# Masking attention scores with a bitwise AND on VectorE, and moving GpSimd's products and low halves of the attention to VectorE

## The chip, the cores and the metric

The kernel runs on one core of a Trainium2 chip. The metric is the device time of one execution in microseconds (us). Engines are named as in the profile: PE is TensorE's matrix multiplication and PEld its weight load, DVE is VectorE, ACT is ScalarE, POOL is GpSimd, SP is SyncE, which only issues DMA transfers here.

## The reference

Three layers follow each other, on 2 sequences of 768 tokens with a model width of 384 (8 heads of 48):

```python
for t in range(S):                       # linear attention with decay
    cur = einsum('bhd,bhe->bhde', u * k[t], v[t])
    y[t] = einsum('bhd,bhde->bhe', r[t], state + cur)
    state = w[t][..., None] * state + einsum('bhd,bhe->bhde', k[t], v[t])
...
u = x + real(fft(fft(x, axis=1), axis=2))          # mixture layer, width 4 * 384
out = u + relu(layernorm(u) @ w_ch1) @ w_ch2
...
h = gelu(x @ w_in); u, v = split(h)                # gated layer, width 1024
out = x + (u * (w_sg @ (layernorm(v) * g) + b_sg)) @ w_out
```

## The kernel before

**Attention in chunks.** The 8 heads of a sequence make 4 pairs, so there are 8 pairs n = 0 to 7 in all: 0 to 3 for the first sequence, 4 to 7 for the second. A pair's 768 tokens are cut into 6 chunks of 128. Within a chunk the decays are undone by a running product, and the chunk becomes three matrix products: scores (keys by queries, of which only those with the key before the query count), the product of the masked scores and the values, and the state carried from chunk to chunk.

For each pair `prep` (lines 199 to 254) loads the decays, the stacked queries and keys (rk) and the values (v) over SP's queue. Then VectorE scans the decays (L232), ScalarE takes a logarithm and an exponential for the reciprocal (L238, L239), a product r*k is formed for the token's own term (L243, only for pairs 0 to 3), VectorE scales the queries (L245), and the keys are made in three steps: a product (L247), a correction of the reciprocal (L249) and the last step (L250). `PV` and `KV` say for which pairs VectorE makes the products of L243 and L247; GpSimd makes the others. Before, these are pair 0 and pairs 0 and 1.

`own_term` (L258 on) gives the term of a token with itself, with u in place of the decay. For pairs 0 to 3 TensorE sums r*k*u over the head (dg_ps), ScalarE copies the 12 columns out of PSUM (L274), and `times_v` multiplies the values by them on GpSimd (L279), which makes dv. For pairs 4 to 7 (`TM`) r, k and u come from memory in another order (prod), GpSimd multiplies them (L264, L266), VectorE sums (L267), and the same `times_v` follows.

`scores` (L282 on) makes three chunks at once for both heads of a pair, so it is called twice per pair and makes 4 tiles of 128x384. Each tile leaves PSUM in a copy by ScalarE (L293) and is masked by GpSimd with an affine select (L294):

```python
nc.scalar.copy(sc, sc_ps)
nc.gpsimd.affine_select(out=sc, in_=sc, pattern=[[0, 3], [1, C]], compare_op=ALU.is_gt, fill=0.0, base=0, channel_multiplier=-1)
```

`chunk_states` transposes the keys (kn), multiplies them by the values (kv_ps), copies these to us, fills dec with the chunks' decays (L317, ScalarE), runs a scan over the chunks on VectorE (L319) and copies the states to U (L321). `values` adds state and score terms in y_ps and adds dv on VectorE (L344). `butterfly` (L346 on) forms sums and differences of the two halves of the tokens (L349, L350), a rounded high half on ScalarE (L351) and the low half as the difference (L352), on GpSimd but for pair 3. The tiles kn, us and the butterfly's x share one buffer (tag "kn", one buffer): each waits until the one before has been read.

**Order.** `attention` (L354 on) runs through the pairs with the loads two pairs ahead. The work of a pair overlaps the tail (the second half of `values` and the butterfly) of the one before. After the first sequence's pairs come the Fourier steps; from there (about 104 us) `merge` interleaves the second sequence's attention with the mixture layer of the first sequence. A planner orders the instructions; each engine then runs its own in that order and waits, in order, for what they need. Manual dependencies (`behind`, `in_order`) keep the order around the end of the first sequence. PSUM has eight banks: five (gps) are taken in turn by scores, z_ps of the mixture layer and other products, and three (cps) hold some of the first sequence's tiles and later the layer's sums.

**Weights.** `convert` (L170 to L172, VectorE) unpacks a weight from 64 bits with shifts and bitwise operations; `divide` splits it into a high half (L176, ScalarE) and a low half (L177, GpSimd). One buffer (st) holds the unpacked words until GpSimd has read them.

Of the kernel before, what the change touches and what calls it, by code (L numbers as in the profile page):

```python
# [9 lines left out]
F32 = mybir.dt.float32  # L10
# [4 lines left out]
U32 = mybir.dt.uint32  # L15
# [8 lines left out]
CFGF = dict(ps=2, su=2)  # L24
KC = 9
LA = 4
KV = range(2)
NJ0 = 28
JP = -1000000
LNPE = ((0, 0),)  # L30
# [1 line left out]
STB = 1  # L32
TB = 0
XB = 1
PV = range(1)
TM = range(4, 8)
YB = 1
DB = 0
# [49 lines left out]
def strided(x, *free):  # L88

    return bass.AP(x.tensor, x.offset, [x.ap[0], *free])  # L90
# [3 lines left out]
def fused(ctx, tc, ins, out, dbg=None):  # L94
# [163 lines left out]
    def own_term(ap, n, b, p, prod, v):  # L258

        dv = ap([C, NC_, 2 * D], "dv")  # L260
        dg = ap([C, NC_, 2, 1], "dg")
        if n in TM:
            r, k, u = (prod[:, i * 2 * D * NC_:(i + 1) * 2 * D * NC_ if i < 2 else ROW].rearrange("p (c e) -> p c e", e=2 * D) for i in range(3))
            own = (nc.vector if n in PV else nc.gpsimd).tensor_tensor(out=r, in0=r, in1=k, op=ALU.mult)  # L264
            behind(own, first_through, mybir.DependencyClass.Sync)
            nc.gpsimd.tensor_tensor(out=r, in0=r, in1=u.to_broadcast([C, NC_, 2 * D]), op=ALU.mult)  # L266
            nc.vector.tensor_reduce(out=dg.rearrange("p c h o -> p (c h o)"), in_=r.rearrange("p c (h e) -> p (c h) e", h=2), op=ALU.add, axis=AX.X)  # L267
            times_v(dv, dg, v)
            return dv
        dg_ps = ps(b, [C, 512], "dg_ps", DB)  # L270
        for c in range(NC_):

            nc.tensor.matmul(dg_ps[:, 2 * c:2 * c + C], lhsT=prod[:, c], rhs=uh[:, None, 2 * p:2 * p + 2].to_broadcast([PR, C // 2, 2]), start=True, stop=True)
        nc.scalar.copy(dg[:, :, :, 0], dg_ps[:, :2 * NC_].rearrange("p (c h) -> p c h", h=2))  # L274
        times_v(dv, dg, v)
        return dv

    def times_v(dv, dg, v):
        nc.gpsimd.tensor_tensor(out=dv.rearrange("p c (h e) -> p (c h) e", h=2), in0=v.rearrange("p c (h e) -> p (c h) e", h=2),  # L279
                                in1=dg.rearrange("p c h o -> p (c h) o").to_broadcast([C, NC_ * 2, D]), op=ALU.mult)  # L280

    def scores(ap, c0, rt, kt):  # L282

        res = []
        sc_pss = [gps.tile([C, 3, C], F32, name="sc_ps", tag="g") for h in range(2)]
        for i, h in [(i, h) for i in range(3) for h in range(2)]:
            c = c0 + i

            hs = slice(64 * h, 64 * h + D)
            nc.tensor.matmul(sc_pss[h][:, i, :], lhsT=kt[hs, c * C:(c + 1) * C], rhs=rt[hs, c, :], start=True, stop=True)  # L290
        for sc_ps in sc_pss:
            sc = ap([C, 3, C], "sc")
            nc.scalar.copy(sc, sc_ps)  # L293
            nc.gpsimd.affine_select(out=sc, in_=sc, pattern=[[0, 3], [1, C]], compare_op=ALU.is_gt, fill=0.0, base=0, channel_multiplier=-1)  # L294
            res.append(sc)
        return res

    def chunk_states(ap, b, ends, kt, v, U):
# [13 lines left out]
                o = c * 2 * D + h * D  # L312
                nc.tensor.matmul(kv_ps[r0:r1, c * D:c * D + C], lhsT=kn[:, c, r0:r1], rhs=vf[:, o:o + C], start=True, stop=True)

        us = ap([PR, D, NC_], "kn")
        nc.scalar.copy(us, kv_ps[:, :NC_ * D].rearrange("p (c e) -> p e c", c=NC_))
        nc.scalar.copy(dec[:, :, 0:NC_ - 1], ends[:, None, 0:NC_ - 1].to_broadcast([PR, D, NC_ - 1]))  # L317
        chain = us.rearrange("p e c -> p (e c)")
        nc.vector.tensor_tensor_scan(out=chain, data0=chain, data1=dec.rearrange("p e c -> p (e c)"), initial=0.0, op0=ALU.add, op1=ALU.mult)  # L319
        for h, r0 in ((0, 0), (1, 64)):  # L320
# [25 lines left out]
    def butterfly(ap, y, AB, es, low):  # L346

        x = ap([C, NC_, 2 * D], "kn")
        nc.vector.tensor_tensor(out=x[:, 0:3], in0=y[:, 0:3], in1=y[:, 3:6], op=ALU.add)  # L349
        nc.vector.tensor_tensor(out=x[:, 3:6], in0=y[:, 0:3], in1=y[:, 3:6], op=ALU.subtract)  # L350
        nc.scalar.copy(AB.hi[:, :, es], x)  # L351
        low.tensor_tensor(out=AB.lo[:, :, es], in0=x, in1=AB.hi[:, :, es].bitcast(F32), op=ALU.subtract)  # L352

    def attention(ap, made, through):  # L354
# [11 lines left out]
        def tail(n, b, p, rt, sc, v, dv):  # L366
            nonlocal gate, region
            if (b, p) == (0, NP - 1):
                region = len(nc.cur_bb.bb.instructions)
            gate = values(b, 3, rt, sc[2:], v, dv, states[n % 2])  # L370
            butterfly(ap, dv, made(b), slice(p * 2 * D, (p + 1) * 2 * D), nc.vector if b == 0 and p == NP - 1 else nc.gpsimd)
            through(b, p)
            return b if p == NP - 1 else None

# [469 lines left out]
    with ExitStack() as main, ExitStack() as low, ExitStack() as late, ExitStack() as att:  # L844
# [4 lines left out]
        nc.gpsimd.memset(d1[:, :, 0:1], 1.0)  # L849
        states = [sh.tile([PR, NC_ - 1, 2 * D], F32, name=f"U{i}") for i in range(2)]  # L850
        all_ends = [sh.tile([PR, NC_], F32, name=f"ends{i}") for i in range(3)]
        dec = sh.tile([PR, D, NC_], F32, name="dec")
        for t in (*states, *all_ends, dec):
            nc.gpsimd.memset(t, 0.0)
        uh = sh.tile([PR, 2 * NP], F32, name="uh")
        dft(sh)

        def load_consts():
            nc.sync.dma_start(out=ident, in_=ins["ident"])
            nc.sync.dma_start(out=uh, in_=ins["uh"])  # L860

        a_room = room(att.enter_context(tc.tile_pool(name="att", bufs=1)), CFG1)
        f1_room = room_of(a_room, ps="v", su="dv")
# [126 lines left out]
def _constants():  # L990
# [15 lines left out]
    for i in range(2):  # L1006
# [5 lines left out]
        "fdft": _parts(fd).transpose(1, 0, 2, 3),  # L1012
        "half": half.reshape(C, 2, 2 * C),
        "ident": np.eye(C, dtype=np.float32),
    }


# [64 lines left out]
```

## Time and profile before

| | |
|---|---|
| median of 3 runs (lowest to highest) | 487.02 us (485.54 to 487.31) |
| the profiled execution's own time, and its span | 485.52 us, 483.7 us |
| PE busy | 433.6 us, 90% of the span, 2662 instructions |
| VectorE busy | 274.0 us, 57%, 453 instructions |
| ScalarE busy | 172.7 us, 36%, 369 instructions |
| GpSimd busy | 182.1 us, 38%, 182 instructions |

The span runs from the first to the last instruction. A share is an average over stages in which different engines set the pace, so it must be read together with the stretches below. A row of the timeline gives the start, the duration, engine, line, operation, and what is written from what; in brackets stands the engine's idle time before it and what ended it. PEclk is the granted clock of TensorE as a part of 2.4 GHz; 0.50 is the lower level, 1.2 GHz.

### The profile page before, as it was taken

How to read it: one execution, taken by the hardware profiler on the slowest of the kernel's cores; microseconds unless marked ns; L12 is line 12 of the kernel's file. 1: busy time of each engine (PE TensorE's matmuls, PEld its weight loads, DVE VectorE, ACT ScalarE, POOL GpSimd, SP SyncE). 2: the span in 40 equal slices, each digit the busy share in tenths (PEclk: the TensorE clock that was granted, in tenths of full speed). 3: DMA queues.
4: the chain of work that ended last, by engine and by line, in shares of the span. 5: the costliest groups of instructions: out<-in, count | busy, mean ns of one | idle time of the engine just before them, and what ended most of it. 6: DMA issues, size and time to landing. Idle time of an engine off the chain costs nothing.

```text
span 483.7 us, 6884 instructions
## 1 busy us (share of the span) xinstructions
PE 433.6 (90%) x2662; PEld 408.3 (84%) x2662; DVE 274.0 (57%) x453; ACT 172.7 (36%) x369; POOL 182.1 (38%) x182
## 2 busy tenths in 40 slices
PE   8778788876789688999999799999998999999994
PEld 8667787765678678899999699999987998999994
DVE  4857387389986978634044963541158734711332
ACT  2435355452344236444322532431355413311110
POOL 2857553154786967320000341200446524200330
PEclk9659899897979989999999899999999999999998
DMA  8948534036035223013000041000243100110002
GB/s 213 251 146 265 166 119 130 0 101 242 0 119 176 91 67 110 1 40 91 1 0 2 1 131 33 1 0 1 66 114 88 61 1 1 43 56 1 0 20 87
DMA packets 14074, 36.75 MB, mean 76 GB/s; under 512 B 1808, under 2 KB 5680, under 8 KB 13648
## 3 DMA queue, kind: packets, MB, share of 16 engines
q1 hardware_dynamic: 13456, 32.54, 22.5%
q0 software_dynamic: 576, 3.68, 2.2%
q8 instruction: 23, 0.38, 0.3%
q14 instruction: 19, 0.16, 0.1%
HBM read 33.86 MB, written 2.36 MB: 75 GB/s over the span
## 4 chain that ended last, share of the span: by engine, by line
PE 55%; DVE 15%; issue 10%; POOL 6%; DMA 5%; ACT 4%; SPq 1%; POOLq 0%; ACTq 0%; DVEq 0%
PE s_ps L107 10%; PE ch L107 8%; PE z_ps L107 8%; PE o_ps L107 5%; PE u_ps L107 4%; PE d_ps L107 3%; PE x_ps L107 3%; PE v_ps L107 3%; PE t_ps L426 2%; PE y_ps L342 2%; DMA raw<-in_wsg 2%; DVE st L171 2%; DVE st L170 2%; DVE st L172 1%; DMA w_raw<-in_w 1%
## 5 line engine op out<-in xcount | busy, mean ns | idle before, releaser
L107 PE MATMUL ch<-z_hi,w 128*128 128x384 f32 x288 | 84.5, 355 | 3.9 <-DVE uT L541 2.3
L107 PE MATMUL z_ps<-us_hi,w 128*128 128x384 f32 x288 | 82.5, 348 | 0.8 <-ACT us_hi L506 0.5
L107 PEld LDWEIGHTS ch<-z_hi,w 128*128 128x128 f32 x288 | 55.4, 199 | 6.0 <-ACT z_hi L530 2.7
L107 PE MATMUL ch<-z_lo,w 128*128 128x384 f32 x144 | 51.3, 356 | 10.2 <-DVE z_lo L531 10.2
L531 DVE SCALAR_TENSOR_TENSOR z_lo<-z_ps,z_hi 128x384 fp32r<-128x384 f32 x48 | 26.4, 552 | 55.7 <-ACT z_hi L530 55.7
L107 PEld LDWEIGHTS z_ps<-us_hi,w 128*128 128x128 f32 x288 | 54.1, 193 | 2.2 <-ACT us_hi L506 0.8
L107 PE MATMUL z_ps<-us_lo,w 128*128 128x384 f32 x144 | 49.4, 343 | 0.0
L530 ACT ACTIVATE z_hi<-z_ps 128x384 fp32r<-128x384 f32 x48 | 23.4, 490 | 57.0 <-PE z_ps L107 43.8
L107 PEld LDWEIGHTS ch<-z_lo,w 128*128 128x128 f32 x144 | 28.5, 198 | 12.4 <-DVE z_lo L531 12.1
L623 POOL TENSOR_TENSOR vn_lo<-t_g,vn_hi 128x384 fp32r<-128x384 f32 x16 | 16.1, 1014 | 57.1 <-ACT vn_hi L622 57.1
L619 DVE SCALAR_TENSOR_TENSOR t_g<-s_ps,g,bsg 128x384 f32<-128x384 f32 x16 | 9.5, 615 | 43.6 <-PE s_ps L107 43.6
L294 POOL TENSOR_SCALAR_AFFINE_SELECT sc<-sc 128x384 f32<-128x384 f32 x32 | 29.5, 939 | 12.0 <-ACT sc L293 12.0
L342 PE MATMUL y_ps<-v,sc 128*128 128x120 f32 (+1 forms) x192 | 34.0, 301 | 0.0
L177 POOL TENSOR_TENSOR w<-st,w 128x384 fp32r<-128x384 f32 (+1 forms) x18 | 24.4, 1363 | 24.0 <-ACT w L176 23.9
L107 PE MATMUL s_ps<-wsg_hi,vn_lo 128*128 128x384 f32 x96 | 32.3, 336 | 0.0
L107 PE MATMUL s_ps<-wsg_hi,vn_hi 128*128 128x384 f32 x96 | 32.3, 336 | 0.0
L107 PE MATMUL s_ps<-wsg_lo,vn_hi 128*128 128x384 f32 x96 | 32.3, 336 | 0.0
L483 POOL TENSOR_TENSOR z_lo<-uc,z_hi 128x384 fp32r<-128x384 f32 x7 | 7.8, 1120 | 60.0 <-ACT z_hi L482 59.9
L342 PEld LDWEIGHTS y_ps<-v,sc 128*128 128x128 f32 x192 | 28.6, 209 | 1.2 <-issue 0.8
L107 PEld LDWEIGHTS z_ps<-us_lo,w 128*128 128x128 f32 x144 | 27.9, 194 | 0.0
L177 POOL TENSOR_TENSOR wsg_lo<-raw,wsg_hi 128x384 fp32r<-128x384 f32 x12 | 12.4, 1038 | 33.2 <-ACT wsg_hi L176 33.2
L622 ACT CAST vn_hi<-t_g 128x384 fp32r<-128x384 f32 x16 | 8.0, 513 | 38.9 <-DVE t_g L620 28.0
(261 smaller groups left out, 1060.0 us busy)
## 6 DMA issues: line engine op xcount, KB each, us to landing
raw<-in_w SPq DMA_DIRECT2D x12, 384.0 KB, 3.4
w_raw<-in_w SPq DMA_DIRECT2D x12, 384.0 KB, 4.5
raw<-in_win SPq DMA_DIRECT2D x8, 384.0 KB, 3.8
prod<-in_ruk SPq DMA_DIRECT2D x4, 624.0 KB, 4.6
tdft<-in_tdft POOLq DMA_DIRECT2D x2, 1158.0 KB, 6.8
v<-in_v SPq DMA_DIRECT2D x8, 288.0 KB, 5.7
raw<-in_wsg SPq DMA_DIRECT2D x12, 192.0 KB, 2.4
out<-o SPq DMA_DIRECT2D x12, 192.0 KB, 1.9
```

The costliest lines, as they stand in the source:

```text
L107: nc.tensor.matmul(o, lhsT=x, rhs=y, start=start and i == 0, stop=stop and i == len(ps) - 1, **kw)
L170: behind(nc.vector.tensor_scalar(out=st, in0=top, scalar1=3, scalar2=0x3FFFFFF8, op0=ALU.logical_shift_left, op1=ALU.bitwise_and), first_t ...
L171: nc.vector.scalar_tensor_tensor(out=st, in0=top, scalar=0xC0000000, in1=st, op0=ALU.bitwise_and, op1=ALU.bitwise_or)
L177: nc.gpsimd.tensor_tensor(out=w.lo[to], in0=x, in1=w.hi[to].bitcast(F32), op=ALU.subtract)
L294: nc.gpsimd.affine_select(out=sc, in_=sc, pattern=[[0, 3], [1, C]], compare_op=ALU.is_gt, fill=0.0, base=0, channel_multiplier=-1)
L342: nc.tensor.matmul(y3[:, i, to], lhsT=sc[h][:, i, :], rhs=vf[:, of], start=c == 0, stop=True, skip_group_check=c > 0)
L426: nc.tensor.matmul(o, lhsT=l, rhs=r, start=i == 0, stop=i == len(parts) - 1)
L530: nc.scalar.activation(out=z.hi, in_=z_ps, func=AF.Relu)
L531: nc.vector.scalar_tensor_tensor(out=z.lo, in0=z_ps, scalar=0.0, in1=z.hi.bitcast(F32), op0=ALU.max, op1=ALU.subtract)
L619: nc.vector.scalar_tensor_tensor(out=t, in0=s_ps[h], scalar=g[:, f:f + 1], in1=bsg[:, hs], op0=ALU.mult, op1=ALU.add)
L622: nc.scalar.copy(vn.hi[:, f, 3 * h:3 * h + 3], th)
L623: nc.gpsimd.tensor_tensor(out=vn.lo[:, f, 3 * h:3 * h + 3], in0=th, in1=vn.hi[:, f, 3 * h:3 * h + 3].bitcast(F32), op=ALU.subtract)
```

## The change

The mask becomes a constant of 128x128 words, all ones where the query comes after the key and zero elsewhere. It is loaded once at the start over SP's queue, behind the identity and uh. The scores' copy and select become one bitwise AND on VectorE that reads PSUM and the mask and writes the masked scores. The own term's multiplication moves from GpSimd to VectorE for all pairs, and for pairs 0 to 3 it reads the 12 columns in PSUM directly, without ScalarE's copy. The products of L247 move to VectorE for pairs 2 to 7, those of L243 for pairs 1 to 3, and the low halves of L352 for all pairs. The tile dec, which stood by itself, becomes the second half of the tile us, is filled whole by ScalarE before the copy of us, and is no longer cleared at the start. The own-term products of pairs 4 to 7 (L264, L266) and the weights' low halves (L177) stay on GpSimd.

```diff
-KV = range(2)
+KV = range(8)
-PV = range(1)
+PV = range(4)
...
-        nc.scalar.copy(dg[:, :, :, 0], dg_ps[:, :2 * NC_].rearrange("p (c h) -> p c h", h=2))
-        times_v(dv, dg, v)
+        times_v(dv, dg_ps[:, :2 * NC_].rearrange("p (c h o) -> p c h o", h=2, o=1), v)
...
     def times_v(dv, dg, v):
-        nc.gpsimd.tensor_tensor(out=dv.rearrange("p c (h e) -> p (c h) e", h=2), in0=v.rearrange("p c (h e) -> p (c h) e", h=2),
+        nc.vector.tensor_tensor(out=dv.rearrange("p c (h e) -> p (c h) e", h=2), in0=v.rearrange("p c (h e) -> p (c h) e", h=2),
...
             sc = ap([C, 3, C], "sc")
-            nc.scalar.copy(sc, sc_ps)
-            nc.gpsimd.affine_select(out=sc, in_=sc, pattern=[[0, 3], [1, C]], compare_op=ALU.is_gt, fill=0.0, base=0, channel_multiplier=-1)
+            nc.vector.tensor_tensor(out=sc.bitcast(U32), in0=sc_ps.bitcast(U32), in1=strided(mask, (0, 3), (1, C)), op=ALU.bitwise_and)
...
-        us = ap([PR, D, NC_], "kn")
+        both = ap([PR, 2, D, NC_], "kn")
+        us, dec = both[:, 0], both[:, 1]
+        nc.scalar.copy(dec, ends[:, None, :].to_broadcast([PR, D, NC_]))
         nc.scalar.copy(us, kv_ps[:, :NC_ * D].rearrange("p (c e) -> p e c", c=NC_))
-        nc.scalar.copy(dec[:, :, 0:NC_ - 1], ends[:, None, 0:NC_ - 1].to_broadcast([PR, D, NC_ - 1]))
...
-            butterfly(ap, dv, made(b), slice(p * 2 * D, (p + 1) * 2 * D), nc.vector if b == 0 and p == NP - 1 else nc.gpsimd)
+            butterfly(ap, dv, made(b), slice(p * 2 * D, (p + 1) * 2 * D), nc.vector)
...
-        dec = sh.tile([PR, D, NC_], F32, name="dec")
-        for t in (*states, *all_ends, dec):
+        for t in (*states, *all_ends):
...
+        mask = sh.tile([C, C], U32, name="mask")
...
             nc.sync.dma_start(out=uh, in_=ins["uh"])
+            nc.sync.dma_start(out=mask, in_=ins["mask"])
...
+        "mask": np.where(p[None, :] > p[:, None], 0xFFFFFFFF, 0).astype(np.uint32),
```

## Rows read from the trace of the kernel before

**Rows 1.** Busy time by stretch: us, then each engine's (instructions), PEclk, DMA share, GB/s.
```profile
23.30:27.30 4.00, 0.00 (x0) 0.00 (x0) 3.93 (x5) 0.14 (x1) 3.44 (x3) 0.50 0.33 83
27.30:35.00 7.70, 7.68 (x45) 6.95 (x46) 4.10 (x3) 4.04 (x9) 3.85 (x4) 0.50 0.45 141
...
49.40:56.80 7.40, 7.26 (x62) 6.29 (x62) 2.67 (x6) 2.73 (x7) 2.82 (x4) 0.77 0.21 61
...
104.00:140.00 36.00, 22.91 (x127) 19.72 (x126) 35.20 (x35) 14.61 (x30) 23.85 (x15) 0.84 0.34 116
140.00:172.00 32.00, 25.42 (x173) 22.16 (x173) 26.52 (x28) 9.90 (x20) 24.65 (x16) 0.97 0.42 144
172.00:216.00 44.00, 41.51 (x304) 38.10 (x301) 27.93 (x55) 21.11 (x46) 21.73 (x20) 0.96 0.17 50
216.00:484.00 268.00, 256.35 (x1447) 249.16 (x1446) 118.00 (x237) 82.18 (x172) 63.27 (x73) 0.99 0.13 38
```

**Rows 2.** Timeline of TensorE, two waits of the first stage.
```profile
27.32 1.01 PE L290 MATMUL sc_ps<-prk 48*128 48x128 f32 x6 [4.09 <-DVE prk L250]
...
49.37 0.98 PE L313 MATMUL kv_ps<-v,kn 128*64 128x128 f32 x10 [3.03 <-ACT kn L305]
```

**Rows 3.** Timeline of VectorE: pair 1's preparation, and instructions of the same sizes later.
```profile
14.54 4.48 DVE L232 TENSOR_TENSOR_SCAN prk<-prk,d 112x774 f32<-112x774 f32 x1
...
21.10 2.50 DVE L247 TENSOR_TENSOR prk<-prk,AL 112x768 f32<-112x768 f32 x1 [0.94 <-ACT AL L239]
...
24.83 2.43 DVE L250 SCALAR_TENSOR_TENSOR prk<-AL,prk 112x768 f32<-112x768 f32 x1
...
104.29 1.75 DVE L232 TENSOR_TENSOR_SCAN P<-P,d 112x774 f32<-112x774 f32 x1
...
116.66 0.94 DVE L250 SCALAR_TENSOR_TENSOR rk<-y,rk 112x768 f32<-112x768 f32 x1
```

**Rows 4.** Timeline of GpSimd in the same time as pair 1's preparation.
```profile
17.35 3.18 POOL L294 TENSOR_SCALAR_AFFINE_SELECT sc<-sc 128x384 f32<-128x384 f32 x2
20.51 1.81 POOL L243 TENSOR_TENSOR AH<-XE 112x768 f32<-112x768 f32 x1
```

**Rows 5.** Timelines of GpSimd and ScalarE before TensorE's wait at 49.4 us.
```profile
45.95 1.54 POOL L247 TENSOR_TENSOR XO<-XO,y 112x768 f32<-112x768 f32 x1
47.45 1.40 POOL L352 TENSOR_TENSOR AL<-kn,AH 128x576 fp32r<-128x576 f32 x1
...
48.88 0.69 ACT L305 COPY kn<-kn_ps 128x336 f32<-128x336 f32 x2 [2.19 <-POOL AL L352]
```

**Rows 6.** Groups by line and shape up to 216 us: busy us, mean ns, idle before.
```profile
L531 DVE SCALAR_TENSOR_TENSOR z_lo<-z_ps,z_hi 128x384 fp32r<-128x384 f32 x15 | 8.2, 549 | 4.4 <-ACT z_hi L530 4.4
L344 DVE TENSOR_TENSOR dv<-y_ps,dv 128x288 f32<-128x288 f32 x16 | 7.1, 444 | 16.4 <-PE y_ps L342 16.4
...
L352 DVE TENSOR_TENSOR AL<-kn,AH 128x576 fp32r<-128x576 f32 x1 | 0.8, 757 | 0.5 <-ACT AH L351 0.5
...
L294 POOL TENSOR_SCALAR_AFFINE_SELECT sc<-sc 128x384 f32<-128x384 f32 x32 | 29.5, 939 | 12.0 <-ACT sc L293 12.0
...
L293 ACT COPY sc<-sc_ps 128x384 f32<-128x384 f32 x32 | 13.7, 480 | 15.6 <-PE sc_ps L290 9.5 <-PE y_ps L342 5.9
```

**Rows 7.** Timeline of SP's queue: the identity's load.
```profile
2.04 0.58 SPq L859 DMA_DIRECT2D ident<-in_ident  x1
```

**Rows 8.** Timelines of VectorE and GpSimd in the second stage.
```profile
113.49 0.54 DVE L170 TENSOR_SCALAR st<-w_raw 128x768 uint32<-128x768 uint32 x1
...
123.20 3.73 DVE L170 TENSOR_SCALAR st<-w_raw 128x768 uint32<-128x768 uint32 x1 [0.66 <-POOL w L177]
...
163.19 2.40 DVE L245 SCALAR_TENSOR_TENSOR rk<-rk,P 112x768 f32<-112x768 f32 x1
...
125.11 1.40 POOL L264 TENSOR_TENSOR prod<-prod 128x576 f32<-128x576 f32 x1
...
161.74 2.56 POOL L247 TENSOR_TENSOR rk<-rk,y 112x768 f32<-112x768 f32 x1
```

## The prediction

> **What bounds the kernel now.** I read the stretches first [rows 1]. From 216 us on TensorE is busy 256 of 268 us, and nothing there is touched by the change. What can move lies before: the first batch's attention (to about 104 us) and the second batch's attention merged with the first mixture layer (104 to 216). In the second stage TensorE works 22.9 + 25.4 + 41.5 = 89.8 of 112 us and so idles for 22; VectorE is busy 35.2 of the 36 us between 104 and 140, and 89.7 of the 112. So there VectorE, with its one queue in program order, sets the pace.
>
> Second, TensorE's timeline for its large waits in the first stage [rows 2]: 4.09 us before 27.3 for the keys of pair 1, which VectorE ends, and 3.03 us before 49.4 for a copy on ScalarE. Third, VectorE's timeline ahead of the first of these [rows 3] against GpSimd's [rows 4]. The same scan, 112x774, takes 4.48 us at 14.5 and 1.75 at 104.3; the key product 2.50 at 21.1 and the last key step 2.43 at 24.8, where an instruction of that size takes 0.94 [rows 3]. While they last GpSimd masks scores and forms products [rows 4]. I read this as two engines in each other's way: VectorE instructions with both inputs in on-chip memory are held up by GpSimd's. Those with one input in PSUM are not: fifteen z_lo average 549 ns and sixteen y_ps additions 444 ns, through stretches in which GpSimd is busy [rows 6]. The new mask and the own term from PSUM are of that kind.
>
> Fourth, what the copy before 49.4 waits for: its buffer is the one that the butterfly's input held until GpSimd had made the low half, and that stood in GpSimd's queue behind the keys of pair 3 [rows 5].
>
> **The change part by part, first stage.**
> Chain to the keys of pair 1. Relief: 4.48 - 1.75 = 2.73, 2.50 - 0.94 = 1.56 and 2.43 - 0.94 = 1.49, together 5.8 us, since every GpSimd instruction of [rows 4] moves. Added on VectorE ahead of the end: the product r*k of pairs 1 and 2 at 0.94 each, pair 0's own term at 0.76 (priced by the low half, same size, [rows 6]), and two to four masks at 0.55: 3.7 to 4.8 us. The 0.94 us that VectorE waits for ScalarE at 21.1 [rows 3] hides one or two of these. So the keys come 1.9 to 3.0 us sooner; if pair 2's product and two masks fall behind, the whole 4.09 us goes. I take -3.0 (ends -1.5 and -4.1).
>
> The wait before 49.4: instead of keys 1.54 and low half 1.40 in GpSimd's queue [rows 5] VectorE needs 0.94 and 0.76, with masks beside them. Take -2.0 (ends 0 and -2.6).
>
> TensorE's clock: behind that wait it was granted 0.77 on average from 49.4 to 56.8 [rows 1], part of it at 1.2 GHz; the work, 7.26 us, would be 5.6 at 2.4 GHz. Without the idle stretch before it some of this comes back: -0.8 (ends 0 and -1.7). Likewise 7.7 us from 27.3 run at 0.50 [rows 1], behind another idle stretch; at 2.4 GHz they would save 3.8. No row shows that closing that wait brings the clock up sooner: 0 in the sum, -3.8 as an end.
>
> The mask's load: 64 KB, as large as the identity's, which SP issues in the same place [rows 7]; behind it stand all of SP's loads of pairs 0 to 3. The identity's takes 0.58 us of SP's queue. Take +0.4 (ends 0 and +0.6). The memset of the dropped tile leaves GpSimd before its first product, where nothing waits for it: 0.
>
> Pairs 2 and 3 and the butterflies: each pair brings VectorE four masks (2.2), keys, own term, low half (0.94 + 0.76 + 0.76), 4.7 us; from 56 us on these stand among the conversions of the weights, and values wait behind masks. Elsewhere VectorE's idle time covers them. Take +1.0 (ends 0 and +2.5).
>
> Sum of the first stage: -3.0 - 2.0 - 0.8 + 0.4 + 1.0 = -4.4.
>
> **The change, second stage.** VectorE gets 4 x 4.7 = 18.6 us. Relief: the conversion at 123.2 takes 3.73 us against 0.54 at 113.5 [rows 8], 3.2 too many, 1.4 of it beside an own-term product (L264) that stays on GpSimd, so 1.8; the key step at 163.2 takes 2.40 against 0.94, 1.5 too many, beside GpSimd's keys, which move. That is 3.3 us as the lower end. Upper end: the three instructions of [rows 3] lose 5.8 us in 9.4 beside GpSimd; if each of the four pairs is relieved as much, 23 in all. Take 10, since GpSimd keeps conversions and own-term products here. Net +8.6 of work, 2 of which fall before 140, where VectorE has no idle time; after it 21.6 us of idle time cover the rest. Against the 2: pair 6's keys, behind which its scores and all that follows stand, take 0.94 instead of 2.56 [rows 8], 1.6 sooner. Take 0, ends -6.5 and +9.6 (both worked out under the rivals).
>
> PSUM: a scores' bank was freed by ScalarE's copy (0.48 us [rows 6], off VectorE's queue); now it is held until VectorE comes to the mask. The five banks are shared with the layer's z_ps, so TensorE's next z waits if a mask is late. That is in the upper end. The decay copy on ScalarE, now before the state's copy and in a part of the same buffer, stays behind the same matmuls: 0. The copies removed leave ScalarE idler; the one wait for it above [rows 2] is GpSimd's in truth: 0.
>
> The mask itself is the one operation that the trace lacks: 128x384, 32 bit, one input in PSUM. Nearest row 549 ns [rows 6]; lower end 444 (288 columns), upper end twice 549 if integers run at half rate: +17.6 us of VectorE over 32 masks. I take 0.55.
>
> By the Trainium skill, Perfetto Trace Analysis, section Optimizing Scalar/DVE Operations, work should leave VectorE for ScalarE or even GpSimd where VectorE is saturated, though between GpSimd and VectorE this may not help, as they share a port. By its first half this change is wrong for 104 to 140, and the time is the slower rival's; by its second half it costs little. The long instructions of [rows 3] beside those of [rows 4] show the sharing.
>
> **Sum.** The profiled execution took 485.5 us, 1.5 below the median of 487.0. 485.5 - 4.4 = 481.1; against the median 482.6. I say 482.5.
>
> **Rivals.**
> Larger gain: the second stage is relieved too. TensorE idles 13.1 + 6.6 us between 104 and 172 [rows 1]; a third of it back is 6.5 us, and the clock's end adds some: 475. For: long collisions stand right before its waits. Against: as much work is added as freed.
> Slower: VectorE is the bound from 104 to 172. If relief is only the 3.3 us shown, 15.3 us are added; six tenths of it (two and a half of four pairs) fall there, 9.6 us, and if the idle time there is waiting in order, unusable, the stage grows by that: 487.0 - 4.4 + 9.6 = 492. It decides as soon as the second stage loses more than the 4.4 gained. For: 61.7 of those 68 us are busy. Against: the collisions of [rows 8].
> No change: the first gain isn't made, because products and masks stand ahead of pair 1's keys and pair 3's low half: only -1.5 and 0 there, nothing of the clock, then +0.4 and +1.0: 487.0 - 0.1 = 486.9. For: one queue in order. Against: 5.8 us of relief on that chain alone.
>
> **Numbers.** Forecast 0.45, its own range 478.5 to 485; larger gain 0.20, slower 0.20, no change 0.15. The likeliest gives 482.5. The range takes in the first two thirds of the way to 475 and 492 and beyond: 474 to 491. Half a per cent is 2.4 us, about what a measurement of this kernel can tell from no change. Faster: nearly all of the forecast and the larger gain, 0.61; same 0.18; slower 0.21.
>
> **What would show it.** Right: the scan of pair 1 near 1.75 us, no 4 us wait of TensorE before pair 1's scores, no wait of a kn copy for a low half; masks at about 0.55 us; VectorE's sum between 104 and 216 up by some 9 us while TensorE's idle time there stays near 22. Wrong: masks near 1.1 us; VectorE's long instructions still long beside L177 and L264; a TensorE wait for a bank that a mask holds; or TensorE's idle time in the second stage off by over 6 us either way.

## The result and the profile after

The changed kernel took 490.1 us at the median, the kernel before beside it 485.28: a ratio of 1.0097, with a 95% interval of 1.0071 to 1.0122. It is slower by 1%, 4.8 us. The forecast was 482.5. Medians from here on leave out executions in a slower state, over 1.5% above the fastest of their kernel; e9's profile is of such a one, so its stretches are not given.

Busy time of the kernel before, cut where the first layer's first output appears (the first z_lo, L531) and at the fifteenth. The columns are those of [rows 1].

```profile
0.00:107.70 107.70, 88.37 (x625) 79.60 (x625) 70.11 (x107) 47.31 (x108) 51.74 (x61) 0.87 0.53 152
107.70:212.40 104.70, 85.22 (x566) 75.91 (x567) 84.11 (x108) 42.72 (x89) 67.05 (x49) 0.92 0.29 97
```

Busy time of the kernel after: the same two stretches, cut at the same two outputs, the rest of its span from 216 us, and three shorter stretches of the first stage:

```profile
0.00:111.40 111.40, 94.90 (x625) 86.46 (x625) 74.53 (x135) 40.42 (x88) 18.34 (x32) 0.81 0.51 147
111.40:216.10 104.70, 87.87 (x567) 78.67 (x568) 87.35 (x134) 37.14 (x73) 36.86 (x22) 0.87 0.30 98
...
216.00:484.00 268.00, 259.92 (x1473) 252.69 (x1472) 120.10 (x243) 82.73 (x174) 62.09 (x72) 0.99 0.13 38
...
15.40:25.70 10.30, 10.01 (x56) 8.36 (x57) 7.83 (x11) 4.11 (x8) 0.00 (x0) 0.50 0.96 239
25.70:35.90 10.20, 8.58 (x51) 7.34 (x52) 9.59 (x14) 2.39 (x5) 1.33 (x2) 0.50 0.37 122
...
40.00:57.00 17.00, 14.83 (x103) 13.26 (x104) 9.66 (x19) 4.68 (x9) 0.00 (x0) 0.70 0.43 129
```

The second stage takes 104.7 us in both, as forecast. The first takes 111.4 instead of 107.7; there the loss is made. From each row two things can be read. TensorE's idle time is length less busy time: 19.3 us before, 16.5 after. What the clock costs is about length times (1 - PEclk): 14.0 before, 21.2 after. What remains, 74.4 and 73.7, is the work at 2.4 GHz, and it is nearly equal. So **TensorE waits 2.8 us less and loses 7.2 us more to its clock.** This reading counts idle time at the lower clock twice; worked out for each microsecond, over busy time alone, the clock costs 11.5 and 18.8 us, 7.3 more. It serves for every run below.

The same stage, cut at the first Fourier product (x_ps) and at the first half transform (t_ps); the first two rows are the kernel before, the last two the kernel after:

```profile
0.00:58.23 58.23, 46.16 (x343) 40.80 (x344) 36.48 (x41) 23.55 (x52) 32.34 (x43) 0.79 0.72 204
58.23:77.83 19.60, 17.02 (x129) 15.62 (x130) 15.25 (x28) 8.48 (x18) 10.21 (x11) 1.00 0.50 150
...
0.00:58.75 58.75, 50.19 (x344) 44.69 (x344) 40.62 (x63) 18.20 (x35) 4.65 (x20) 0.74 0.68 190
58.75:81.82 23.07, 19.67 (x130) 18.80 (x131) 15.84 (x34) 7.40 (x15) 4.54 (x4) 0.85 0.51 161
```

Up to the Fourier product TensorE idles 3.5 us less after the change, but the clock costs 3.1 more; the kernel is 0.5 us behind. From there to the half transform it loses 3.5 us, nearly all of it to the clock (0.85 against 1.00).

TensorE's larger waits in the first stage of the kernel after (timeline; these answer to [rows 2]):

```profile
15.56 0.64 PE L303 MATMUL kn_ps<-ident,rk 112*128 112x112 f32 x2 [3.20 <-DVE rk L250]
...
28.95 1.65 PE L289 MATMUL sc_ps<-prk 48*128 48x128 f32 x12 [1.62 <-DVE prk L250]
...
39.88 0.94 PE L289 MATMUL sc_ps<-XE 48*128 48x128 f32 x12
...
43.43 1.64 PE L289 MATMUL sc_ps<-XE 48*128 48x128 f32 x6 [2.17 <-DVE sc L293]
...
70.37 0.74 PE L333 MATMUL y_ps<-U,XO 112*128 112x96 f32 x2 [3.40 <-ACT U L321]
```

Pair 2's first scores in the kernel before, and its row for 40 to 57 us:

```profile
40.47 0.94 PE L290 MATMUL sc_ps<-XE 48*128 48x128 f32 x12
```

```profile
40.00:57.00 17.00, 13.64 (x121) 11.73 (x119) 9.83 (x13) 9.21 (x20) 10.29 (x11) 0.90 0.65 201
```

The wait before 49.4 is gone. In its place stand one of 2.17 us at 43.4 for a mask, behind which 40 to 57 us run at 0.70 of the clock (0.90 before), and one of 3.40 at 70.4. A wait of 3.20 us ends at 15.6 (1.56 us before, ending at 14.7); it is for pair 0's last key step, which now stands on VectorE behind pair 0's own term and pair 1's product. Pair 1's scores start at 28.95, later than the 27.32 of [rows 2], but pair 2's start at 39.88, 0.6 us sooner than before. From 12 to 36 us the clock is the same in both kernels (0.58 and 0.57); what it costs more comes behind the waits at 43.4 and 70.4.

Timeline of VectorE of the kernel after, pair 1's preparation (compare [rows 3]) and, from 35.67, pair 3's:

```profile
14.07 0.96 DVE L243 TENSOR_TENSOR AH<-prk 112x768 f32<-112x768 f32 x1 [0.29 <-DMA prk<-in_rk]
...
15.42 1.76 DVE L232 TENSOR_TENSOR_SCAN prk<-prk,d 112x774 f32<-112x774 f32 x1
...
19.31 0.96 DVE L243 TENSOR_TENSOR AH<-XE 112x768 f32<-112x768 f32 x1 [0.35 <-DMA XE<-in_rk]
...
21.12 0.95 DVE L247 TENSOR_TENSOR prk<-prk,AL 112x768 f32<-112x768 f32 x1
22.26 0.76 DVE L319 TENSOR_TENSOR_SCAN kn<-kn 112x288 f32<-112x288 f32 x1 [0.20 <-ACT kn L317]
24.34 0.76 DVE L278 TENSOR_TENSOR dv<-v,dg_ps 128x576 f32<-128x576 f32 x1 [1.32 <-PE dg_ps L273]
25.82 0.96 DVE L243 TENSOR_TENSOR prod<-XO 112x768 f32<-112x768 f32 x1 [0.73 <-DMA XO<-in_rk]
...
27.57 0.45 DVE L344 TENSOR_TENSOR dv<-y_ps,dv 128x288 f32<-128x288 f32 x1
27.95 0.95 DVE L250 SCALAR_TENSOR_TENSOR prk<-AL,prk 112x768 f32<-112x768 f32 x1
...
35.67 1.76 DVE L232 TENSOR_TENSOR_SCAN XO<-XO,d 112x774 f32<-112x774 f32 x1
...
41.30 0.96 DVE L250 SCALAR_TENSOR_TENSOR XO<-y,XO 112x768 f32<-112x768 f32 x1
42.18 0.75 DVE L319 TENSOR_TENSOR_SCAN kn<-kn 112x288 f32<-112x288 f32 x1
42.84 0.53 DVE L293 TENSOR_TENSOR sc<-sc_ps,mask 128x384 uint32<-128x384 uint32 x1
```

The relief came in full: the scan takes 1.76 us instead of 4.48, the key product 0.95 instead of 2.50, the last key step 0.95 instead of 2.43. But ahead of that last step the queue now holds pair 1's own term, which waits 1.32 us for TensorE, and the product r*k of pair 3, which waits 0.73 us for a load. Before, GpSimd waited for that load (0.56 us, until 24.54), with none of pair 1's keys behind it; in VectorE's queue everything stands behind it. The mask that TensorE waits for at 43.43 stands behind all of pair 3's steps.

The masks themselves, all of them (least/median/most ns, first and last start):

```profile
L293 DVE TENSOR_TENSOR sc<-sc_ps,mask x32: 530/546/558, 17.1 to 212.3; 128x384 uint32<-128x384 uint32 x32
```

They cost what was taken for them, 0.55 us each, 17.5 in all, also where GpSimd works beside them.

### The profile page after: what moved, and what is told of

Same layout as the page of the kernel before. It is cut to its first block, busy times and chain, and to the rows that moved or that the text cites. A ratio compares the mean times of both kernels' runs of the same rounds, so it can differ in the third digit from the quotient of the medians.

```text
span 486.7 us, 6814 instructions
## 1 busy us (share of the span) xinstructions
PE 442.6 (91%) x2662; PEld 417.7 (86%) x2662; DVE 281.9 (58%) x509; ACT 160.2 (33%) x333; POOL 117.3 (24%) x125
## 3 DMA queue, kind: packets, MB, share of 16 engines
q1 hardware_dynamic: 13600, 32.60, 22.3%
## 4 chain that ended last, share of the span: by engine, by line
PE 59%; DVE 16%; DMA 10%; issue 8%; ACT 3%; POOL 2%; SPq 1%; POOLq 0%; ACTq 0%; DVEq 0%
PE s_ps L107 10%; PE ch L107 9%; PE z_ps L107 9%; PE o_ps L107 5%; PE u_ps L107 4%; PE x_ps L107 4%; DMA XO<-in_rk 3%; PE y_ps L342 3%; PE d_ps L107 3%; PE t_ps L426 3%; PE v_ps L107 3%; DMA raw<-in_wsg 2%; PE sc_ps L289 2%; PE y_ps L333 2%; DMA raw<-in_w 2%
## 5 line engine op out<-in xcount | busy, mean ns | idle before, releaser
L531 DVE SCALAR_TENSOR_TENSOR z_lo<-z_ps,z_hi 128x384 fp32r<-128x384 f32 x48 | 26.4, 552 | 58.4 <-ACT z_hi L530 58.4
L177 POOL TENSOR_TENSOR w<-st,w 128x384 fp32r<-128x384 f32 (+1 forms) x18 | 26.7, 1484 | 82.1 <-ACT w L176 82.1
L530 ACT ACTIVATE z_hi<-z_ps 128x384 fp32r<-128x384 f32 x48 | 23.4, 489 | 60.6 <-PE z_ps L107 46.6
L342 PE MATMUL y_ps<-v,sc 128*128 128x120 f32 (+1 forms) x192 | 35.8, 317 | 0.0
L342 PEld LDWEIGHTS y_ps<-v,sc 128*128 128x128 f32 x192 | 31.1, 226 | 0.6 <-issue 0.3
L623 POOL TENSOR_TENSOR vn_lo<-t_g,vn_hi 128x384 fp32r<-128x384 f32 x16 | 16.1, 1014 | 57.0 <-ACT vn_hi L622 57.0
L483 POOL TENSOR_TENSOR z_lo<-uc,z_hi 128x384 fp32r<-128x384 f32 x7 | 9.5, 1351 | 76.3 <-ACT z_hi L482 70.7
L293 DVE TENSOR_TENSOR sc<-sc_ps,mask 128x384 uint32<-128x384 uint32 x32 | 16.9, 546 | 7.2 <-PE sc_ps L289 4.4
L177 POOL TENSOR_TENSOR wsg_lo<-raw,wsg_hi 128x384 fp32r<-128x384 f32 x12 | 12.3, 1036 | 32.8 <-ACT wsg_hi L176 32.7
```

Source lines behind the costliest of these rows:

```text
L177: nc.gpsimd.tensor_tensor(out=w.lo[to], in0=x, in1=w.hi[to].bitcast(F32), op=ALU.subtract)
L293: nc.vector.tensor_tensor(out=sc.bitcast(U32), in0=sc_ps.bitcast(U32), in1=strided(mask, (0, 3), (1, C)), op=ALU.bitwise_and)
L342: nc.tensor.matmul(y3[:, i, to], lhsT=sc[h][:, i, :], rhs=vf[:, of], start=c == 0, stop=True, skip_group_check=c > 0)
L483: nc.gpsimd.tensor_tensor(out=parts.lo, in0=x, in1=parts.hi.bitcast(F32), op=ALU.subtract)
L530: nc.scalar.activation(out=z.hi, in_=z_ps, func=AF.Relu)
L531: nc.vector.scalar_tensor_tensor(out=z.lo, in0=z_ps, scalar=0.0, in1=z.hi.bitcast(F32), op0=ALU.max, op1=ALU.subtract)
```

## The experiments

Each kernel was timed beside the kernel before on the same chip (483.6 to 485.0 us there). A planner makes a new order for every kernel, so a single edit moves other instructions too. The columns from "first stage" on are worked out from one profiled execution's row, as above; its time differs from the kernel's median by up to 4.4 us (e11: 487.8 against 483.4; e5 3.6 below, e3 3.5 above), so only large differences between rows count.

| kernel | median us | ratio (95%) | first stage | idle | clock | second stage |
|---|---|---|---|---|---|---|
| before | 485.3 | | 107.7 | 19.3 | 14.0 | 104.7 |
| after | 490.1 | 1.010 (1.007-1.012) | 111.4 | 16.5 | 21.2 | 104.7 |
| e1 moves only | 477.2 | 0.983 (0.975-0.991) | 103.8 | 18.3 | 12.5 | 103.1 |
| e2 masks only | 494.2 | 1.018 (1.011-1.025) | 116.3 | 22.3 | 18.6 | 105.5 |
| e3 both edges | 480.1 | 0.989 (0.983-0.996) | 102.6 | 16.1 | 8.2 | 108.6 |
| e4 filler | 483.3 | 0.999 (0.995-1.003) | 107.0 | 17.3 | 8.6 | 102.8 |
| e5 copy, then AND | 487.7 | 1.007 (1.002-1.013) | 104.6 | 19.6 | 8.4 | 106.5 |
| e6 weights first | 488.0 | 1.008 (1.002-1.013) | 106.4 | 15.5 | 14.9 | 108.9 |
| e7 both edges, filler | 473.5 | 0.981 (0.975-0.987) | 96.8 | 11.6 | 1.9 | 104.7 |
| e8 moves only, filler | 481.0 | 0.995 (0.990-0.999) | 101.9 | 15.4 | 5.1 | 106.5 |
| e9 before, filler | 483.8 | 1.000 (0.996-1.005) | - | - | - | - |
| e10 both edges, filler, old masks | 478.7 | 0.986 (0.979-0.993) | 104.2 | 16.8 | 5.2 | 102.7 |
| e11 own-term edge | 483.4 | 0.998 (0.993-1.003) | 109.6 | 18.0 | 17.5 | 105.5 |
| e12 product edges | 479.3 | 0.989 (0.986-0.992) | 100.7 | 13.8 | 10.1 | 105.0 |
| e13 one product back | 481.4 | 0.994 (0.990-0.997) | 103.5 | 14.8 | 13.5 | 102.7 |
| e14 product edges, old masks | 476.5 | 0.981 (0.973-0.988) | 101.7 | 13.3 | 14.2 | 103.0 |
| e15 product edges, filler | 475.1 | 0.980 (0.974-0.986) | 99.3 | 10.6 | 5.0 | 102.2 |
| e16 product edges, masks twice | 493.2 | 1.018 (1.012-1.025) | 114.8 | 16.9 | 20.7 | 105.4 |
| e17 masks first | 490.0 | 1.011 (1.006-1.017) | 111.7 | 19.6 | 16.8 | 108.0 |
| e18 masks first, weights first | 491.2 | 1.012 (1.005-1.019) | 111.9 | 18.5 | 19.0 | 107.9 |

Length less idle less clock is 73 to 78 us in the first stage of every kernel in the table, and 81 to 84 where filler was added.

### e1 and e2: the two halves of the change

e1 is the kernel after with the masks as before; e2 is the kernel before with the masks, their load and the decays beside us. The diff is e1's, against after; e2's is the reverse, against before.

```diff
-            nc.vector.tensor_tensor(out=sc.bitcast(U32), in0=sc_ps.bitcast(U32), in1=strided(mask, (0, 3), (1, C)), op=ALU.bitwise_and)
+            nc.scalar.copy(sc, sc_ps)
+            nc.gpsimd.affine_select(out=sc, in_=sc, pattern=[[0, 3], [1, C]], compare_op=ALU.is_gt, fill=0.0, base=0, channel_multiplier=-1)
```

> The changed kernel with the old masks: ScalarE's copy and GpSimd's select instead of the AND; all the moved products, keys and lows stay on VectorE. Queue theory (products and own terms that wait for a load or for TensorE stand in VectorE's queue ahead of pair 1's keys): still slower than before, 488 us or more, and TensorE begins pair 1's scores after 27 us. Mask theory (the AND is what costs: VectorE time, PSUM banks held until it is done): back at 485 or below. Clock theory (the waits got shorter in sum, but the granted clock is at its lower level for longer): time follows the half-clock time in the first 216 us, 50 us of it before, 68 after, half a us each.

> The kernel before with the masks alone moved (AND on VectorE, the mask's load, dec inside us to make room for it). Mask theory: as slow as the change, 489 to 491. Queue theory: pair 1's scores begin before 25 us, since no product stands ahead of its keys and GpSimd's selects are gone; 480 to 485. Clock theory: as the half-clock time goes.

The moves gain 1.7%, the masks lose 1.8%: the loss comes with the masks, although each takes only 0.55 us. The order changes with them, though: in e1 pair 3's product stands behind pair 1's last key step (27.48 and 24.31), in the kernel after ahead of it. In e2 pair 1's scores begin at 24.4, the 3 us sooner that the masks' leaving GpSimd should give, and the stage is yet 8.6 us longer; 7.9 of these lie between the first Fourier product (58.9) and the half transform (86.4), where the kernel after loses 3.5.

### e3, e4 and e7: the order and the clock at the start

In e3 the products and pair 1's own term are put behind key steps (ready_k[1] is pair 0's last key step, ready_k[2] pair 1's); e4 has more of the dummy columns that TensorE works on while it waits; e7 has both. First the diff of e3, then that of e4, each against after:

```diff
+                if n:
+                    behind(product, ready_k[1 if n == 1 else 2])
...
+        if n == 1:
+            behind(own, ready_k[2])
```

```diff
-NJ0 = 28
+NJ0 = 44
```

> The changed kernel with three order edges on VectorE's queue: the product of pair 1 behind pair 0's last key step, the products of pairs 2 and 3 and the own term of pair 1 behind pair 1's last key step. Nothing is added or taken away. Queue theory: pair 1's scores begin by 26 us instead of 29, and the time falls by 2 to 4 us, to 486 to 488. Mask theory: no change beyond 1 us. Clock theory: falls only if the half-clock time does.

> The changed kernel with 44 instead of 28 dummy products at the start, so that TensorE works through its wait before pair 0's last transposes (12 to 15 us) and a part of the one before pair 1's scores. No wait of another engine is shortened. Clock theory: the stretch at the lower clock that begins at 15 us and lasts to 36 gets shorter or goes, and the time falls by 3 to 6 us. Queue and mask theory: the same time within 1.5 us.

> The changed kernel with both the three order edges of e3 and the 44 dummy products of e4. If both act on the same stretch at the lower clock (15 to 36 us): no faster than e3, 479 to 481. If the edges shorten waits and the filler raises the clock apart from that: 475 to 478.

e3 brings 480.1, 10 us less than after where its queue theory expected 2 to 4, with the clock term down from 21.2 to 8.2; pair 1's scores begin at 25.0. e4 shows the clock; these are the stretches of e4 in which the kernel after ran at 0.50:

```profile
15.40:25.70 10.30, 6.02 (x60) 5.04 (x60) 8.05 (x12) 2.77 (x6) 0.00 (x0) 1.00 1.02 239
25.70:35.90 10.20, 7.67 (x45) 6.94 (x46) 8.50 (x11) 3.62 (x7) 1.33 (x2) 0.50 0.51 169
```

With the dummies ahead of it TensorE keeps 2.4 GHz to 25.7; its wait for pair 0's last key step is 1.64 us instead of 3.20, and 60 products, ten of them dummies, take 6.0 us where 56 took 10.0. Pair 1's scores begin at 28.2. e7, with 473.5 us, is the fastest of all and has every mask on VectorE. An AND has no fixed price, then.

### e5 and e6: a bank, a load

In e5 ScalarE empties the bank as before and VectorE makes the AND from the copy in place. In e6 pair 4's 624 KB of own-term operands are loaded behind the first two loads of weights, which VectorE waits for 2.45 us in after.

Their diffs against after:

```diff
-            nc.vector.tensor_tensor(out=sc.bitcast(U32), in0=sc_ps.bitcast(U32), in1=strided(mask, (0, 3), (1, C)), op=ALU.bitwise_and)
+            nc.scalar.copy(sc, sc_ps)
+            nc.vector.tensor_tensor(out=sc.bitcast(U32), in0=sc.bitcast(U32), in1=strided(mask, (0, 3), (1, C)), op=ALU.bitwise_and)
```

```diff
+            first_w.append(nc.sync.dma_start(out=raw, in_=src[:, o:o + NST]))
...
+            if n == 4:
+                behind(ruk, first_w[1])
```

> The changed kernel with ScalarE's copy of the scores kept and the AND on VectorE reading that copy in place, so that a scores bank in PSUM is free after the copy, while VectorE has the same 32 masks. Bank theory (TensorE waits for banks that a late mask holds): most of the masks' cost goes, 478 to 483 us, and no TensorE wait for scores of pair 2 near 43 us. Queue theory (what costs is where the masks and the rest stand in VectorE's queue): still 487 to 492.

> The changed kernel with one order edge on SP's queue: the load of pair 4's own-term operands (624 KB) behind the first two weight loads instead of ahead of them. If that load is what makes VectorE wait 2.45 us for a weight at 62 us, and with it TensorE 3.4 us at 67 to 70: that wait goes or falls below 1.5 us, and the time falls by 2 to 4 us, to 486 to 488. If the order in VectorE's queue before 45 us is all: the same time within 1.5 us.

The banks are not the main cause: e5's copies free them, TensorE waits 5.00 us at 41.6 for a state instead, and the time is the queue theory's. e6 does not decide: TensorE's wait of 3.40 falls to 2.21, but VectorE's for the weight only from 2.45 to 2.25, and its time, 488.0, can't be told from that of after.

### e8 and e9: filler elsewhere

The same edit, in e8 on e1 and in e9 on the kernel before:

```diff
-NJ0 = 28
+NJ0 = 44
```

> The masks back on ScalarE and GpSimd as in e1, and 44 dummy products. There the low stretch begins at 14.7 us and lasts 10 us, behind a TensorE wait of 3.8 us that the dummies fill. Clock theory: a part of the 5 us that half a clock costs comes back, 473 to 475.5. Queue theory: as e1, 477 within 1.5.

> The kernel before with only its dummy columns ahead of the first scores raised from 28 to 44 groups. If the filler's gain with the edges (480.1 to 473.5) is a gain of TensorE's clock at the start and has nothing to do with the change: before gains as much, 5 to 7 us, to about 477. If the filler only pays where the keys of pair 1 come early (behind them TensorE has work to do at the higher clock): before's keys of pair 1 come at 27 whatever the filler, and the time stays within 2.5 us of before.

Filler gives nothing to e9, and e8 is 3.7 us slower than e1: the clock term falls there (12.5 to 5.1), but the dummies are work of their own, 8 us more in the stage. e8's expectation was missed. Early keys are not what makes filler pay: e8's scores of pair 1 begin at 24.5, e4's, where it paid 6.8 us, at 28.2. It paid in the three kernels with the masks on VectorE (e4 6.8, e7 6.6 over e3, e15 4.2 over e12, to 475.1 where 472 to 475 was expected) and in neither of these two with the masks on GpSimd. Why is open.

### e11 and e12: which edge

Each has one half of e3's diff, against after: e11 that of the own term, e12 that of the products.

```diff
+        if n == 1:
+            behind(own, ready_k[2])
```

```diff
+                if n:
+                    behind(product, ready_k[1 if n == 1 else 2])
```

> The kernel after with one of the edges: pair 1's own term behind pair 1's last key step; the products stay where the planner puts them. If the wait for TensorE (1.32 us at 24.3 ahead of the own term, and 0.76 for it) is most of the 2.6 to 4.7 us lost in that queue: pair 1's scores begin at about 26.5 to 27 instead of 28.9, and the time is at 484 to 486. If the products behind loads carry it, the scores stay near 28.5 and the time at 489 to 490.

> The kernel after with the other edges alone: the product of pair 1 behind pair 0's last key step, those of pairs 2 and 3 behind pair 1's last key step; pair 1's own term stays where the planner puts it. If the products (0.95 and 0.73 of waiting at 25.8, and 0.29 ahead of pair 0's last key step) carry it: pair 1's scores begin at about 26.5 to 27, and the time is at 483 to 486. If the own term carries it, the scores stay near 28 and the time at 488 to 490.

In e11 VectorE reaches the product sooner and waits there 2.51 us for the load, so the scores start at 29.1. VectorE's timeline of e11:

```profile
26.21 0.96 DVE L243 TENSOR_TENSOR prod<-XO 112x768 f32<-112x768 f32 x1 [2.51 <-DMA XO<-in_rk]
```

Yet e11 takes 483.4, some 6 us less than after, though its scores start no sooner and the product still stands ahead of the keys. Neither of its two expectations had that. In e12, VectorE's timeline:

```profile
13.99 1.76 DVE L232 TENSOR_TENSOR_SCAN prk<-prk,d 112x774 f32<-112x774 f32 x1
...
20.79 0.73 DVE L280 TENSOR_TENSOR dv<-v,dg_ps 128x576 f32<-128x576 f32 x1
21.43 0.95 DVE L251 SCALAR_TENSOR_TENSOR AL<-prk,AL 112x768 f32<-112x768 f32 x1
...
22.42 0.96 DVE L252 SCALAR_TENSOR_TENSOR prk<-AL,prk 112x768 f32<-112x768 f32 x1
...
25.83 0.95 DVE L243 TENSOR_TENSOR prod<-XO 112x768 f32<-112x768 f32 x1
```

The keys are done at 23.4, the product runs at 25.8 as before and waits for nothing, and even pair 1's own term stands ahead of the keys without a wait. The products' edges alone give all that e3 gained, more than was expected of them; but as e11 shows, the own term's edge alone gives more than half of it, so the two do not add up.

### e10, e14 and e16: the masks where the order is right

e10 and e14 are e7 and e12 with e1's diff. e16 is e12 with each mask made twice, into the same tile:

```diff
+            nc.vector.tensor_tensor(out=sc.bitcast(U32), in0=sc_ps.bitcast(U32), in1=strided(mask, (0, 3), (1, C)), op=ALU.bitwise_and)
```

> The kernel after with the order edges and 44 groups of dummies, and the masks on ScalarE and GpSimd as before: the fastest version so far with the masks undone. Theory 1 (the AND is cheap wherever VectorE's queue has the room, and only the order made it dear): same as the version with AND, 473.5, within 2.5 us. Theory 2 (the masks cost some 10 us on VectorE whatever the order, as between the moves alone and the whole change): about 464. Theory 3 (masks on GpSimd slow VectorE's key steps beside them, so that the AND pays once the order is right): slower, 477 to 480.

> The kernel after with the product edges and the masks on ScalarE and GpSimd as before. Theory 1 (the AND costs nothing of itself; the 13 us between the whole change and the moves alone were the product's wait and the clock behind it): same as the product edges with AND, 479.3, within 2.5 us. Theory 2 (the masks' 16.9 us on VectorE cost some 10 us in any order): 468 to 472. Theory 3 (without the AND GpSimd's masks slow VectorE's key steps): slower than 482.

> The kernel after with the product edges, and each mask made twice (the same AND from the same bank into the same tile again): 32 more instructions of 0.55 us on VectorE, 17.5 us in sum, half of them in the first stage. If VectorE has room for the masks behind the keys: up to 3 us more than 479.3. If VectorE's time for masks goes onto the path as the masks alone on before suggest (8.7 us for 16.9): 487 to 491.

The masks on VectorE cost 13 us on the moves (e1 to after) and 8.7 on before (e2), but 2.8 on the product edges (e14 to e12), a little more than its first theory allowed, and with edges and filler they gain 5 (e10 to e7), as the third theory of e10 had it; in these last two pairs the intervals overlap. The second set of masks in e16 costs 13.9 us, more than either theory expected, and not evenly: the first stage takes 16 of them, 8.5 us, and grows by 14.1, of which the clock term is 10.6 and idle time 3.1; the second stage takes the other 16 and grows by 0.4. So no price per microsecond of VectorE's time comes out. That the first set costs less because it also takes GpSimd's selects away is not shown.

### e13, e17 and e18: one instruction

e13 gives only pair 3's product back to GpSimd. e17 leaves it and puts pair 3's key product behind the masks of pair 1's second scores; e18 adds e6's edit. The diffs of e13 and e17 against after:

```diff
-PV = range(4)
+PV = range(3)
```

```diff
+            if n == 3:
+                behind(step, masks[6])
+                behind(step, masks[7])
```

> The kernel after with one instruction taken back: the product r*k of pair 3, which in after stands in VectorE's queue ahead of pair 1's last two key steps and waits there for a load, goes to GpSimd as in the kernel before. The rest of the early order stays nearly as in after, the own term of pair 1 still ahead of those key steps. If that product is the step that costs the change its gain: pair 1's scores begin 1.7 to 2.5 us sooner than in after (26.5 to 27.2 instead of 28.9) and the time comes to 479 to 484, as with the order edges. If the gain of those edges came from the new order elsewhere: 488 to 490, as after.

> The kernel after with one order edge: pair 3's key product (the third last of its preparation on VectorE) behind the two masks of pair 1's second scores. Pair 3's product r*k stays ahead of pair 1's keys as in after, so pair 1's scores should begin at 28.9 as there. Late-mask theory (the loss is made at 43.4, where TensorE waits 2.17 us for a PSUM bank until a mask behind five of pair 3's steps is done, and then works 10.2 us at the lower clock): that wait goes, the 16.4 us from pair 2's first scores to pair 3's become 9 to 12, and the time is 481 to 484, though pair 1's keys are as late as in after. Late-keys theory (the loss is the 1.6 us by which pair 1's scores start later than before, and the clock behind that): 488 to 491, as after.

> The edge of the masks, and on SP's queue the load of pair 4's own-term operands behind the first two loads of weights. From the first Fourier product (58.8 in after) to the first half transform (81.8) after takes 23.1 us and before 19.6; VectorE waits there 2.45 us for a weight's load ahead of pair 3's state scan, and TensorE 3.40 for the state. If that wait is a second loss of its own: 2 to 4 us below the version with the edge of the masks alone. If it is hidden by what follows (the time from there to the first layer output is the same): within 1.5 us of it.

e13 takes 481.4: one instruction is worth 8.7 us. Its time was expected, its way was not. VectorE's timeline of e13:

```profile
25.05 0.95 DVE L249 SCALAR_TENSOR_TENSOR AL<-prk,AL 112x768 f32<-112x768 f32 x1
...
26.04 2.44 DVE L250 SCALAR_TENSOR_TENSOR prk<-AL,prk 112x768 f32<-112x768 f32 x1
```

GpSimd's timeline of e13:

```profile
25.14 2.53 POOL L243 TENSOR_TENSOR prod<-XO 112x768 f32<-112x768 f32 x1 [22.35 <-DMA XO<-in_rk]
```

Busy time of e13 by stretch:

```profile
40.00:57.00 17.00, 16.56 (x169) 15.17 (x166) 12.47 (x24) 6.49 (x14) 0.00 (x0) 1.00 0.88 276
```

The product on GpSimd collides with pair 1's last key step, and the scores begin at 28.5, only 0.4 us sooner. The gain is made at 40 to 57: TensorE works almost without a wait at the full clock where after has 0.70, and reaches the first Fourier product at 51.0 instead of 58.75. The planner has put the masks ahead of pair 3's last steps there. e17 was to show whether that alone does it. It does not: the wait at 43.4 goes, pair 3's first scores come at 51.7 instead of 56.2, and by the first half transform (82.1 against 81.8) all is given back, in waits of 1.39 us at 63.0 and 2.44 at 74.3. e18 is 1.3 us above e17, as expected if the weights' load is no loss of its own; but VectorE's wait for the first weight did not shrink (3.50 us at 60.5, in e17 1.93 at 58.7 and 0.65 at 60.9), so this stays untested. Busy time of e17 by stretch:

```profile
40.00:57.00 17.00, 12.84 (x123) 11.12 (x123) 12.33 (x23) 5.40 (x11) 0.00 (x0) 0.99 0.80 245
57.00:82.00 25.00, 20.39 (x125) 18.95 (x125) 18.88 (x36) 8.18 (x17) 4.54 (x5) 0.80 0.38 123
```

**What the runs show.** Pair 3's product given back to GpSimd (e13), or the products put behind the key steps (e12), makes up more than the whole loss. Among the kernels with the moves and a single set of masks, those in which pair 3's product stands ahead of pair 1's last key step on VectorE take 483.3 us or more (after, e4, e5, e6, e11, e17, e18); those in which it stands behind that step or on GpSimd take 481.4 or less (e1, e3, e7, e8, e10, e12 to e15). This sorting was made afterwards and its gap is narrow: e4 and e11 lie within the spread of e13's executions (479.3 to 486.4), and both are 6 to 7 us faster than after with the product where it was. **What stays open** is the path from there to the clock: neither the start of pair 1's scores (e13, e11) nor the late mask (e17) carries it alone, and the planner's new orders could not be held still. Why the masks alone lose 8.7 us on the kernel before, where the product is on GpSimd, is open too.

## Why the prediction was wrong

**Chain to the keys of pair 1, -3.0: this step failed.** The relief was right (2.72 + 1.55 + 1.48 us of the 5.8). What was added was priced by duration alone, "3.7 to 4.8 us", and the list was short. Four instructions stood there that it does not name, 2.9 us: pair 1's own term, pair 3's product, pair 0's state scan (22.26) and an addition (27.57). And the step never asked when inputs arrive: VectorE waits 0.29, 0.35, 0.20, 1.32 and 0.73 us in that queue, 2.9 again. The scores came 1.6 us later instead of 3.0 sooner. With the products put behind (e12) they come at 25.1, 2.2 us sooner. The rival "no change" named this mechanism, products ahead of the keys in an in-order queue, with a chance of 0.15, but stopped at no gain. The Trainium skill, PSUM — Partial Sum Buffer, section Engine vs sequencer instructions, says that VectorE's queue is strictly first in, first out; the rows at 24.34 and 25.82 agree.

**TensorE's clock, -0.8: this step failed too, in sign and size, and it carries the number.** The clock cost 7.2 us more; that is 8.0 of the 8.1 us between the forecast for the first stage, -4.4, and the measured +3.7. The term looked only at the stretch behind the wait that would go, not at the new waits that would come; after has them at 43.4 and 70.4. How far the late keys led to these waits is open: pair 2's scores were no longer late, and e17 took away the first of the two without a gain.

**The wait before 49.4, -2.0.** It went, as argued, and a wait for a mask took its place; idle time fell by 3.5 us up to the first Fourier product, against the 5.0 of this term and the keys' together, and by 2.8 in the whole stage.

**Pairs 2 and 3, +1.0.** From the first Fourier product to the first half transform after takes 23.1 us (58.75 to 81.82) and before 19.6 (58.23 to 77.83): +3.5, beyond the upper end of 2.5; 3.5 of clock and 0.8 of waiting, less 0.8 of the rest.

**Second stage, 0.** Measured 104.7 and 104.7, in part by luck. The row above shows its two sides: VectorE's busy time rose by only 3.2 us for 18.6 of added work, where 8.6 was taken, so the relief was about 15, between the ends of 3.3 and 23. TensorE idled 2.7 us less (19.5 to 16.8), and its clock cost 5.2 more (0.92 to 0.87), which no term named. This is not tried by a run of its own.

**The mask, 0.55.** 0.546 measured. **Its load, +0.4:** pair 0's first scores start at 10.3 instead of 11.1, so no cost shows there; the loads behind it were issued up to 0.8 us later, and what that costs was not tried.

The rival that VectorE is the bound was placed in the second stage; there it did not decide, and that its 492 lies near the 490.1 is luck. e16 shows that VectorE's time can cost more than its length in the first. The rule drawn on in the prediction (the Trainium skill, Perfetto Trace Analysis, section Optimizing Scalar/DVE Operations) leaves both ways open between GpSimd and VectorE; e1 and e2 show one of each within one change. The prediction's own reading, that VectorE instructions with both inputs in on-chip memory are held up by GpSimd's, holds for some only; the last section has two that were not.

## What to carry to other kernels

When work moves to another engine, its waits move too: for each instruction look up when its operands land and what will stand behind it, and if something critical does, try the order the other way round. Read each stage as work, idle time and clock; a change that removes waits can still lose by where the remaining ones fall. Take the parts of a change one by one before it is dropped: here the same masks and moves with an order edge and 16 more dummies are 1.9% faster than the kernel before (e7).

## What the runs showed of the hardware

The AND of 128x384 words took 546 ns from PSUM (kernel after) and 550 ns from SBUF (median of 32 in e5), never over 559, beside busy and idle GpSimd alike: in e5 two of them from SBUF took 1.02 us together at 158.0, beside a GpSimd instruction (L177) that lasted from 157.3 to 161.4. One GpSimd product, itself 2.53 us long where such a product took 1.81 in [rows 4], stood beside two VectorE key steps in e13: the last, of 0.95 us elsewhere, took 2.44, while the correction before it (L249, at 25.05) took its usual 0.95. In the kernel after, 20.5 us from 15.4, behind a wait of 3.20 us, ran at 1.2 GHz while TensorE was busy for 10.0 of the first 10.3 us of them; with 16 more groups of dummies before, and a wait of 1.64, the same first stretch ran at 2.4 GHz (e4).
